# Block-sparse attention with a feed-forward layer: the preparation of the second sequence is issued in earlier steps

## The chip, the cores and the metric

One core of a Trainium2 chip runs the whole computation. Its engines work side by side and are told apart in the profile as PE (matmuls), PEld (the loading of weights into PE), DVE (VectorE), ACT (ScalarE), POOL (GpSimd) and SP (SyncE, which here issues nearly all transfers). The metric is the time of one execution on the device in microseconds (us). Lower is better. Every time below is of this kernel on one core, and "L723" is line 723 of the kernel.

## The reference

Four sequences of 768 positions, eight heads of 64 dimensions. Attention is block-sparse in blocks of 32: each block of queries sees its neighbours, the first and the last block, and three sampled blocks; the first and the last block of queries see everything. The heads are then joined to 512 features per position and go through two matrices with a leaky rectifier between them.

```python
def _attn_ref(q, k, v, sampled_blocks):
    ...
    scores = scale * np.matmul(q, k.transpose(0, 1, 3, 2))
    ...
    mask = np.abs(blk_i - blk_j) <= window
    mask = mask | (blk_i == 0) | (blk_j == 0) | (blk_i == n_blocks - 1) | (blk_j == n_blocks - 1)
    for qb in range(n_blocks):
        for kb in sampled_blocks[qb]:
            mask[qb * block:(qb + 1) * block, kb * block:(kb + 1) * block] = True
    ...
    attn = np.exp(scores)
    attn = attn / (np.sum(attn, axis=-1, keepdims=True) + 1e-09)
    return np.matmul(attn, v).astype(np.float32)

def _moe_ref(x, w_in, w_out):
    h = x @ w_in
    g = np.maximum(0.01 * h, h)
    return (g @ w_out).astype(np.float32)
```

The inputs and the result are float32. The kernel splits each operand into a high and a low float16 half and multiplies the halves, which is where most of its preparation comes from.

## The kernel before

**Steps.** The work is a list of 192 steps. A step is one unit: 64 queries of two heads (a head pair, `hp` 0 to 3) of one tile. Four head pairs make a tile (`T`), four tiles make an item, three items make a sequence, so a sequence is 48 steps: the first has steps 0 to 47, the second begins with step 48. For every unit PE forms scores (L714), DVE subtracts the mask and takes the maximum (L723), ACT takes the exponential (L735) and the high half of the normalised weights (L762), DVE the low half (L783), one transfer turns a pair of units around (L788), and PE multiplies by V (L815). Tile 0 of a sequence (steps 48 to 51 in the second) sees all 768 keys, so it needs no gathered keys but takes two parts per unit; each later tile works on 384 gathered keys.

**What a sequence needs beforehand.** Each of these is a Python generator that issues one piece and then yields a cost in "units" (about a microsecond of ACT or DVE each):

- queries, `prep_q`: half an item at a time, 128 positions, halves 0 to 23; halves 6 to 11 are the second sequence's. A square on ACT (L230), a sum across partitions on PE (L135), a scale on DVE (L149 to L158), the high half on ACT (L594), the low half on DVE (L596), a transposing transfer (L599) and two copies (L601, L602). The raw half is loaded by `load_q` into a single buffer.
- keys, `prep_k`: one head pair at a time, with the same pieces (L230, L135, L149 to L158, L564, L568, L570) and one transposing transfer into the tile `kt` (L574). The buffer of the split keys, `k16`, is single, so the next head pair's square waits for this one's transfer; the raw keys have two buffers. `kt` shares two buffers with `wbuf`, in which raw weights are decoded, so the second sequence's `kt` takes over the place of the first one's.
- values, `prep_v`: four squares, one sum, one scale, and then for each head pair the high half (L505), two low halves (L508) and a transfer to DRAM (L512), from which later tiles gather rows (L676, L683).
- weights, `prep_weights`: eight parts, decoded from raw words (L363 to L367) and split (L430, L435, L425 to L428). A credit of 1.8, 1.7 and from step 32 on 4.5 units a step sets how fast they are issued.

`gather_k` builds the keys of a tile: one DVE copy (L647) and six POOL copies (L656), issued from the step in which the tile before it begins. `start_gather` forces all four head pairs' keys to be complete first.

**The order.** A string of letters per step says in which order the pieces of a step are issued (`ord` up to step 47, `ord1` from step 48); "p" stands for `side_step`, "S" for the scores of the following units. `side_step` has a quota of 1.6 units in steps below 16 and of 1.2 units after that. It goes once through the list of open flows, queries first and the others in the order in which they were opened, and takes one piece from each as long as quota is left. A flow that is needed and not complete is forced through at that place (`until`). A scheduler then puts the instructions on the engines' queues by priority, 200 apart per step, as their inputs are ready in its own model of time; squares and sums of the weights have a priority 1500 higher. Each engine works through its queue in order, and so does SP's queue of transfers.

**The feed-forward part** comes in chunks (`ffn_h` L850, `ffn_o` L877), eight per item and 24 matmuls of L850 in each. The first two items go quarter by quarter as the weights' quarters are ready; from step 48 on one chunk is issued in every second step, by a table of due steps.

**The places that the change touches** are the driver loop (the calls of `start_q`, `get_k` and `start_k`), the line of "p" in it, and the sort in `side_step`. In the kernel before, the second sequence's keys are loaded in steps 26, 31, 36 and 41 and opened in 29, 34, 39 and 44; its first queries (half 6) are loaded in step 35 and opened in step 40; its values are loaded in 28 to 34 and opened in step 36.

Of the kernel before, what the change touches and what calls it, by code (L numbers as in the profile page):

```python
# [29 lines left out]
CFG = {  # L30
    "ahead": 3,
    "av_lag": 3,
    "bs": 1500,
    "early": 2,
    "even_at": 48,
    "even": 12,
    "flag": 1,
    "g": 2,
# [20 lines left out]
    "rmin": 0.0,  # L59
    "side": 1.2,  # L60
    "side0": 1.6,
    "spair": 1,
    "spread": 8,
    "v_at": 28,
# [8 lines left out]
def tile_block_sparse_attention_ffn(  # L73
# [508 lines left out]
    def prep_q(b, j, i, rq):  # L582

        nm = f"q{b}_{j}_{i}"
        ss = sm.tile([P, 1], F32, tag="ssq", name=f"ss_{nm}")
        qa = pa.tile([P, H, 2, D], F16, tag="qa", name=f"qa_{nm}", bufs=1)
        square(flat(qa)[:, :H * D], rq.rearrange("p h d -> p (h d)"), ss)
        yield 0.7
        yield 0.01
        pb = scale_sum(ss, 1, nm)  # L590
        yield 0.2
        inv, s = scale_of(pb, 1, nm)
        yield 0.4
        nc.scalar.activation(qa[:, :, 1, :], rq, AF.Copy, scale=s[:, :1])  # L594
        yield 0.7
        nc.vector.scalar_tensor_tensor(  # L596
            out=qa[:, :, 0, :], in0=rq, scalar=s[:, :1], in1=qa[:, :, 1, :], op0=ALU.mult, op1=ALU.subtract)
        qs = pa.tile([P, H, P], F16, tag="qs", name=f"qs_{nm}", bufs=2)
        nc.sync.dma_start_transpose(out=qs, in_=flat(qa))  # L599
        qxs = pa.tile([P, H, P], F16, tag="qxs", name=f"qxs_{nm}", bufs=2)  # L600
        nc.sync.dma_start(out=qxs[:D], in_=qs[D:])  # L601
        nc.sync.dma_start(out=qxs[D:], in_=qs[:D])  # L602
        last_sp["q"] = latest()
        qstack[b, j, i] = (qs, qxs, inv)
        yield 0.8
# [323 lines left out]
    flows = []  # L929

    def start(key, gen):
        gens[key] = gen
        flows.append(key)
# [21 lines left out]
    def side_step(amount):  # L955

        quota[0] = min(quota[0] + amount, 2 * amount)
        for key in sorted(flows, key=lambda a: a[0] != "q"):
            if quota[0] <= 0:
                break  # L960
            c = next(gens[key], "end")
            if c == "end":
                flows.remove(key)
            else:
                quota[0] -= c or 1.0
# [61 lines left out]
    def get_q(n):  # L1027
        if n < len(halves):
            if n >= CFG["rq"]:
                until(("q", *halves[n - CFG["rq"]]), lambda: halves[n - CFG["rq"]] in qstack)  # L1030
            rq[n] = load_q(*halves[n])

    def start_q(n):
        if n < len(halves):
            start(("q", *halves[n]), prep_q(*halves[n], rq[n]))
# [8 lines left out]
    def start_k(b, hp):  # L1044
        start(("k", b, hp), prep_k(b, hp, rk[b, hp]))
# [48 lines left out]
    step = 0  # L1094
# [44 lines left out]
    for u in units:  # L1139
        it, ui = u.item, u.k * NP + u.hp  # L1140
        b, nb = it.b, it.b + 1
# [2 lines left out]
            start_q(1)  # L1144
        if step == 6 or step % 8 == 3 and step > 8:
            get_q((step + 5) // 8 + 1)
        if step % 8 == CFG["q_at"] % 8:
            start_q(step // 8 + (2 if CFG["q_at"] < 8 else 1))
        if nb < B:
            g = it.j * 16 + ui  # L1150
            t = g - (CFG["k_at"] if b else CFG["k_at0"])
            every = CFG["k_every"] if b else 5
            if t % every == 0 and 0 <= t // every < NP:
                get_k(nb, t // every)
            if t % every == every - 2 and 0 <= t // every < NP:
                start_k(nb, t // every)
            t = g - CFG["v_at"]
            if t in (0, 2, 4, 6):
                load_v(nb, t // 2)
            if t == 8:  # L1160
                start(("v", nb), prep_v(nb))
# [18 lines left out]
        for w in CFG["ord1" if step >= CFG["ord1_at"] else "ord"]:  # L1180
            if w == "c" and c:
                ffn_act1(c)
            elif w == "m" and c:
                ffn_max(c)
            elif w == "g" and c:
                ffn_act2(c)
                oq.append(aq.popleft())
            elif w == "S" and step + 1 < len(units):
                ahead = units[step + 1:step + 3]
                if not CFG["spair"]:  # L1190
                    scores(ahead[:1])
                elif u.pi == 1:
                    if any(x.parts > 1 for x in ahead):
                        for x in ahead[:1]:
                            scores([x])
                    else:
                        scores(ahead)
                elif u.parts > 1:
                    scores(ahead[:1])
            elif w == "t":  # L1200
                while live[0] + u.parts > CFG["p"]:
                    if not pend_high and not pend_split:
                        norm_step()
                    high_step()
                    split_step()
                live[0] += u.parts
                unit_ttr(u)
            elif w == "x":
                unit_exp(u)
                if step >= CFG["even_at"]:  # L1210
                    last_exp[0] = latest()
                if u.pi == 1:
                    pend_norm.append(u.pair)
            elif w == "d":
                norm_step()
            elif w == "i":
                high_step()
            elif w == "s":
                split_step()
            elif w == "a":  # L1220
                av_step()
                if vq and vfree[0] and (vq[0][0], "ready") in scr:
                    start_gather_v()
            elif w == "v":
                ev_step()
            elif w == "b":
                do_out()
            elif w == "o":
                do_o(CFG["flag"] if hq or aq else 0)
            elif w == "p":  # L1230
                side_step(CFG["side0"] if step < 16 else CFG["side"])
                gather_step(2)
            elif w == "w":
                wcredit += [r for a, r in CFG["wr"] if step >= a][-1]
                now = tc.cur_priority
                if step < 16:
                    tc.cur_priority = now + CFG["wlate"]
                begin = len(nc.cur_bb.bb.instructions)
                while wcredit >= 1.0:
                    c = next(weights, "end")  # L1240
                    wcredit -= c if c != "end" else wcredit
                if 0 < step < 16:
                    behind(begin, last_ttr[0])
                tc.cur_priority = now
            elif w == "h":
                for i in range(n):
                    if i:
                        do_act()
                        do_o(CFG["flag"])
                    do_h()  # L1250
# [65 lines left out]
```

## Time and profile before

| | us |
|---|---|
| median of three runs | 850.7 |
| the three runs | 850.25 to 853.37 |
| the profiled execution, as timed | 851.52 |
| its span in the profile | 849.8 |

The profile belongs to the execution of 851.52 us: 849.8 us from the first to the last instruction, and 1.7 us around it. That execution is 0.8 us above the median of the three runs. The tables of windows in the prediction give, for each stretch of the span, how many of its microseconds an engine was busy, the number of instructions in brackets, the clock granted to TensorE as a share of full speed, and the mean busy share of the transfer engines (it can be over 1).

### The profile page before, as it was taken

How to read it: one execution, taken by the hardware profiler on the slowest of the kernel's cores; microseconds unless marked ns; L12 is line 12 of the kernel's file. 1: busy time of each engine (PE TensorE's matmuls, PEld its weight loads, DVE VectorE, ACT ScalarE, POOL GpSimd, SP SyncE). 2: the span in 40 equal slices, each digit the busy share in tenths (PEclk: the TensorE clock that was granted, in tenths of full speed). 3: DMA queues.
4: the chain of work that ended last, by engine and by line, in shares of the span. 5: the costliest groups of instructions: out<-in, count | busy, mean ns of one | idle time of the engine just before them, and what ended most of it. 6: DMA issues, size and time to landing. Idle time of an engine off the chain costs nothing.

```text
span 849.8 us, 20081 instructions
## 1 busy us (share of the span) xinstructions
PE 749.3 (88%) x7140; PEld 500.6 (59%) x7140; DVE 595.5 (70%) x1595; ACT 507.6 (60%) x1199; POOL 352.8 (42%) x472
## 2 busy tenths in 40 slices
PE   1666675857798999999999999998999999999997
PEld 1455543545465666666666666665666666667664
DVE  5768889898777976867777777678666776651221
ACT  5757678776445766767566667675657556551211
POOL 0218356433233464646343455454244545332221
PEclk9977778989799999999999999999999999999999
DMA  9979289998756999996969999969586766662000
GB/s 198 273 218 247 73 176 240 245 260 147 168 131 106 175 213 190 203 179 146 197 154 154 196 182 186 202 130 204 119 155 150 125 149 139 125 129 35 26 1 25
DMA packets 312004, 135.33 MB, mean 159 GB/s; under 512 B 279774, under 2 KB 292063, under 8 KB 311903
## 3 DMA queue, kind: packets, MB, share of 16 engines
q1 hardware_dynamic: 305262, 113.59, 67.2%
q0 software_dynamic: 6640, 20.45, 9.3%
q8 instruction: 56, 0.92, 0.5%
q14 instruction: 46, 0.37, 0.2%
HBM read 65.58 MB, written 12.58 MB: 92 GB/s over the span
## 4 chain that ended last, share of the span: by engine, by line
PE 70%; DMA 12%; DVE 10%; issue 3%; ACT 2%; SPq 2%; POOL 0%; POOLq 0%; ACTq 0%; DVEq 0%
PE h L850 27%; PE o L877 26%; PE s L714 8%; PE av L815 7%; DMA pt<-pp 3%; DMA wbuf<-in_moe_w_out_dram 2%; DMA qxs_q<-qs_q 2%; DMA qs_q<-qa_q 2%; DVE p L723 2%; DVE pp L783 2%; PE turn L773 2%; DVE W L365 1%; DVE W L435 1%; DVE W L367 1%; PE q_sum L135 1%
## 5 line engine op out<-in xcount | busy, mean ns | idle before, releaser
L877 PE MATMUL o<-W,g 128*128 128x512 f16 x1152 | 270.9, 381 | 6.4 <-DVE ob L898 4.2
L850 PE MATMUL h<-x,W 128*128 128x256 f16 x2304 | 274.2, 277 | 0.2 <-DVE x L833 0.2
L850 PEld LDWEIGHTS <-W 128*128 128x128 f16 x2304 | 225.0, 100 | 37.7 <-issue 3.9
L864 POOL TENSOR_TENSOR g<-ht,g 128x512 f16<-128x512 f32 x96 | 116.9, 1217 | 304.5 <-DVE g L863 254.6
L735 ACT ACTIVATE p<-p,mx 128x384 f32<-128x384 f32 x208 | 126.2, 607 | 158.7 <-DVE mx L723 123.0
L877 PEld LDWEIGHTS <-g 128*128 128x128 f16 x1152 | 108.7, 98 | 125.6 <-issue 10.8
L656 POOL COPY kg<-kt 128x256 f16 x264 | 135.0, 540 | 45.0 <-issue 15.4
L783 DVE SCALAR_TENSOR_TENSOR pp<-p,r,pp 128x384 f16<-128x384 f32 x188 | 120.4, 666 | 24.9 <-ACT pp L762 23.6
L762 ACT ACTIVATE pp<-p,r 128x384 f16<-128x384 f32 x188 | 104.2, 604 | 23.9 <-DVE r L747 10.2
L723 DVE CUSTOM_DVE_ANT_0 p<-s,em,nsc 128x384 f32<-128x384 f32 x176 | 102.0, 608 | 19.8 <-PE s L714 17.1
L683 POOL DMA_INDIRECT vg<-scr,rows x88 | 91.3, 1037 | 50.4 <-issue 20.3
L859 DVE SCALAR_TENSOR_TENSOR ht<-ht 128x512 f32<-128x512 f32 x96 | 67.8, 706 | 53.3 <-ACT ht L856 52.7
L815 PE MATMUL av<-pt,vg 128*64 128x128 f16 x2112 | 82.1, 226 | 10.1 <-DMA pt<-pp 9.6
L815 PEld LDWEIGHTS <-vg 128*64 128x64 f16 x2112 | 73.4, 114 | 27.4 <-issue 21.7
L714 PE MATMUL s<-kg,qs_q 128*64 128x384 f16 x352 | 66.2, 351 | 25.0 <-DVE mx L723 22.7
L856 ACT ACTIVATE ht<-h,gd 128x512 f32<-128x512 f32 x80 | 53.8, 672 | 57.3 <-PE h L850 54.7
L714 PEld LDWEIGHTS <-qs_q 128*64 128x64 f16 x416 | 27.0, 111 | 79.2 <-issue 53.7
L714 PE MATMUL s<-kg,qxs_q 128*64 128x384 f16 x352 | 64.0, 343 | 5.4 <-DMA qxs_q<-qs_q 5.4
L747 DVE RECIPROCAL r<-sum 128x2 f32<-128x2 f32 x96 | 15.4, 161 | 60.2 <-ACT sum L746 57.8
L863 DVE CAST g<-ht 128x512 f16<-128x512 f32 x96 | 41.8, 435 | 9.4 <-PE o L877 7.2
L735 ACT ACTIVATION_READ_ACCUMULATOR p<-p,mx 128x1 f32 x208 | 39.0, 187 | 0.0
L714 PEld LDWEIGHTS <-qxs_q 128*64 128x64 f16 x416 | 26.2, 114 | 20.8 <-DMA qxs_q<-qs_q 9.7
(138 smaller groups left out, 758.0 us busy)
## 6 DMA issues: line engine op xcount, KB each, us to landing
vg<-scr SPq DMA_DIRECT2D x33, 256.0 KB
qxs_q<-qs_q SPq DMA_DIRECT2D x48, 128.0 KB
v<-in_v_dram SPq DMA_DIRECT2D x32, 192.0 KB
scr<-v SPq DMA_DIRECT2D x16, 384.0 KB
W<-in_moe_w_in_dram SPq DMA_DIRECT2D x5, 1024.0 KB
rq<-in_q_dram SPq DMA_DIRECT2D x20, 256.0 KB
out_dram<-ob SPq DMA_DIRECT2D x20, 256.0 KB
rk<-in_k_dram SPq DMA_DIRECT2D x24, 192.0 KB
```

Source lines behind the costliest of these rows:

```text
L656: nc.gpsimd.tensor_copy(out=kg[:, :, slot * BLOCK:(slot + 1) * BLOCK], in_=kt[:, :, bass.ds(off, BLOCK)])
L683: nc.gpsimd.indirect_dma_start(out=vg[:n_, c, :], out_offset=None, in_=scr[b][:, :], in_offset=bass.IndirectOffsetOnAxis(ap=rows[:n_, c - ...
L714: nc.tensor.matmul(o, a, k, start=(n == 0), stop=(n == 1)))
L723: nc.vector.tensor_tensor_reduce(out=u.p[i], in0=u.sp[i], in1=kgs[u.b, u.T][1] if u.T else zero.to_broadcast([P, KEYS]), scale=u.nsc, scal ...
L735: nc.scalar.activation(u.p[i], u.p[i], AF.Exp, scale=-1.0, bias=u.mx[:, :1], accum_out=u.pair.sum[:, u.pi, i:i + 1])
L762: nc.scalar.activation(pp[:, 0, :], p, AF.Copy, scale=u.r)
L783: nc.vector.scalar_tensor_tensor(out=pp[:, 1, :], in0=p, scalar=u.r, in1=pp[:, 0, :], op0=ALU.mult, op1=ALU.subtract)
L815: nc.tensor.matmul(o, a, m, start=(c == 0 and l == 0), stop=(c == n - 1 and l == 1)))
L850: nc.tensor.matmul(c.ph[:, i], w, x, start=(d == 0 and m == 0), stop=(d == NP - 1 and m == 2)))
L859: nc.vector.scalar_tensor_tensor(out=c.t, in0=c.t, scalar=0.01, in1=c.t, op0=ALU.mult, op1=ALU.max)
L864: nc.gpsimd.tensor_tensor(out=c.g[:, 1], in0=c.t, in1=c.g[:, 0], op=ALU.subtract)
L877: nc.tensor.matmul(o, a, w, start=(c.first and i == 0 and m == 0), stop=(c.last and i == 1 and m == 2)))
```

## The change

- A setting `side1` of 2.0 is added: `side_step` gets a quota of 2.0 units in steps 28 to 47, where it had 1.2.
- The open flows are taken in the order queries, keys, values; before, queries came first and the others in the order in which they were opened.
- The second sequence's keys are loaded every four steps (26, 30, 34, 38) and opened in steps 28, 32, 36 and 40.
- Half 6 of the queries is opened in step 37 in place of 40. The other halves are opened in the steps that they had.

Nothing is added to or taken from what is computed; instructions are issued in another order.

```diff
+    "side1": 2.0,
...
     def side_step(amount):
 
         quota[0] = min(quota[0] + amount, 2 * amount)
-        for key in sorted(flows, key=lambda a: a[0] != "q"):
+        for key in sorted(flows, key=lambda a: "qkv".index(a[0])):
             if quota[0] <= 0:
                 break
             c = next(gens[key], "end")
...
-        if step % 8 == CFG["q_at"] % 8:
-            start_q(step // 8 + (2 if CFG["q_at"] < 8 else 1))
+
+        if step == 37:
+            start_q(6)
+        elif step % 8 == 0 and step != 40:
+            start_q(step // 8 + 1)
         if nb < B:
             g = it.j * 16 + ui
             t = g - (CFG["k_at"] if b else CFG["k_at0"])
-            every = CFG["k_every"] if b else 5
+            every = CFG["k_every"] if b else 4
...
             elif w == "p":
-                side_step(CFG["side0"] if step < 16 else CFG["side"])
+                side_step(CFG["side0"] if step < 16 else CFG["side1"] if 28 <= step < 48 else CFG["side"])
                 gather_step(2)
```

## The prediction

> **What bounds the kernel now.** First the page's busy shares, where PE is the busiest engine with 88%, then windows of the span, stage by stage. I cut them where the scores (next fence) show a border.
>
> ```profile
> span 849.8 us, 20081 instructions
> PE 749.3 (88%) x7140; PEld 500.6 (59%) x7140; DVE 595.5 (70%) x1595; ACT 507.6 (60%) x1199; POOL 352.8 (42%) x472
> ```
> ```profile
> core 0: us, PE busy (x) PEld busy (x) DVE busy (x) ACT busy (x) POOL busy (x), PEclk, DMA share, GB/s
> 137.00:196.00 59.00, 35.31 (x380) 24.06 (x380) 55.93 (x150) 46.92 (x109) 25.27 (x31) 0.86 1.14 239
> 196.00:246.00 50.00, 42.45 (x371) 29.13 (x370) 38.23 (x100) 23.78 (x44) 13.32 (x12) 0.90 0.77 150
> 246.00:284.00 38.00, 33.15 (x308) 19.30 (x308) 29.91 (x83) 22.73 (x59) 15.84 (x25) 0.96 0.59 115
> 284.00:300.00 16.00, 16.00 (x161) 11.06 (x161) 15.64 (x43) 10.78 (x26) 6.39 (x9) 1.00 0.99 183
> 300.00:850.00 550.00, 538.56 (x5166) 357.58 (x5163) 347.76 (x922) 314.07 (x762) 238.74 (x314) 1.00 0.72 142
> ...
> 370.00:458.00 88.00, 86.66 (x890) 57.14 (x888) 65.54 (x178) 59.50 (x147) 38.62 (x51) 1.00 0.84 170
> 565.00:653.00 88.00, 84.02 (x836) 54.79 (x834) 63.79 (x171) 56.13 (x136) 37.43 (x51) 0.98 0.74 158
> ...
> 196.00:284.00 88.00, 75.59 (x677) 48.43 (x674) 68.14 (x183) 46.52 (x102) 29.16 (x36) 0.92 0.69 135
> ```
>
> From 300 us on PE is busy for 538.56 of 550 us: whatever is won ahead of that comes out of the end nearly whole, since the same matmuls follow. In 137 to 196 (steps 28 to 47 by the order of L723) DVE is the bound: 55.93 of 59 us. Between them lies the change of sequences: in 196 to 284 PE idles 12.41 us (88 − 75.59) at a clock of 0.92. The two later changes of sequence, in windows as long, idle 1.34 and 3.98 us at 1.00 and 0.98. Those sequences are prepared well ahead; the second is not. Its scores show that:
>
> ```profile
> 192.86 0.33 PE L714 MATMUL s<-kg,qxs_q 128*64 128x384 f16 x2
> ```
> ```profile
> 227.19 0.58 PE L135 MATMUL wo_sum<-wo_ss,ones 128*128 128x1 f32 x2 [1.14 <-DVE wo_ss L204]
> 227.64 0.56 PE L135 MATMUL q_sum<-ss_q,ones 128*128 128x1 f32 x2
> ...
> 233.14 0.42 PE L135 MATMUL k_sum<-ss_k,ones 128*128 128x1 f32 x2
> 245.93 0.35 PE L714 MATMUL s<-kt,qs_q 128*64 128x384 f16 x2
> ```
> ```profile
> 173.41 0.62 ACT L230 ACTIVATE qa_q<-rq 128x512 f16<-128x512 f32 x1
> ...
> 195.74 0.83 ACT L230 ACTIVATE k_k<-rk 128x768 f16<-128x768 f32 x1
> ...
> 245.65 0.84 ACT L230 ACTIVATE k_k<-rk 128x768 f16<-128x768 f32 x1 [2.31 <-DMA kt<-k_k]
> ```
>
> For 53.1 us (192.86 to 245.93) no score is formed. Half 6 was squared at 173.41, but its sum runs at 227.64, in PE's queue right behind a weight sum which itself waited for DVE. The third head pair of keys was squared at 195.74 and summed only at 233.14; the fourth is squared at 245.65, behind the third's transfer. The transfers say what holds each:
>
> ```profile
> 169.00 5.41 POOL L656 COPY kg<-kt 128x256 f16 x6
> ```
> ```profile
> 175.53 2.12 SPq L574 DMA_TRANSPOSE kt<-k_k  x1
> ...
> 188.60 2.37 SPq L574 DMA_TRANSPOSE kt<-k_k  x1
> ...
> 224.72 5.23 SPq L512 DMA_DIRECT2D scr<-v  x3
> ...
> 235.37 1.23 SPq L599 DMA_TRANSPOSE qs_q<-qa_q  x1
> ...
> 240.19 1.51 SPq L602 DMA_DIRECT2D qxs_q<-qs_q  x1
> 241.75 1.56 SPq L574 DMA_TRANSPOSE kt<-k_k  x1
> ...
> 255.30 1.45 SPq L574 DMA_TRANSPOSE kt<-k_k  x1
> ```
>
> The first keys of the second sequence land right behind the first sequence's last gather (169.00 + 5.41 = 174.41, then 175.53): `kt` takes over that buffer. The four then follow each other through the single `k16`: 13.1 us from the first to the second, 53.2 to the third, 13.6 to the fourth.
>
> **The change part by part.** I counted by hand in which step each piece is issued; a flow gives one piece per pass at most.
>
> *Queries.* Half 6: square 40 → 37, sum 42 → 39, low half and transfers 43 → 42. On PE, sums and feed-forward chunks go in order of step as banks come free: the keys' sum of step 36 ran at 183.57, that of V (step 41) at 202.84, half 6's (step 42) at 227.64.
>
> ```profile
> 183.57 0.38 PE L135 MATMUL k_sum<-ss_k,ones 128*128 128x1 f32 x2 [0.85 <-ACT k_k L230]
> ...
> 202.84 0.28 PE L135 MATMUL v_sum<-ssv,ones 128*128 128x4 f32 x2
> ```
>
> Step 39 lies between the first two: some 195. From sum to first score the chain took 18.3 us (227.64 to 245.93), so the scores would begin near 213, 33 us sooner.
>
> *Keys.* Last pieces: 34, 39, 48, 48 → 33, 37, 41, 45; the forced run of seven pieces in step 48 goes. The first cannot land sooner than the last gather allows (175), the second follows at about 188 as now, and the third's square at 195.74 stays. Only its sum no longer waits 37 us; at 13.1 us a head pair (first to second) the third lands near 202 and the fourth near 215, where they took 241.75 and 255.30. Loading every four steps buys little: the raw keys have two buffers, and the fourth load waits for the second's low half anyway. Each load is 192 KB twice either way; it moves by 2 to 3 steps on a queue of transfers that is 1.14 busy in that window. I cost it at 0; bounds are −1 and +2.4 us (one transposing transfer of keys on SP, 2.37).
>
> *Values.* Last piece 51 → 49, and keys go first. The rate of 2.0 can't do more for them: one piece a pass from step 36 ends in step 49. V's last transfers were issued by 230 (224.72 + 5.23), and the first that needs V is this:
>
> ```profile
> 270.51 0.61 PE L815 MATMUL av<-pt,v 128*64 128x128 f16 x15 [0.65 <-DMA pt<-pp]
> ```
>
>  Thirty-three us sooner that would be 237, still behind V's 230. Cost 0, between −1 and +2 us by the same rows.
>
> *What is moved into the full stage.* What leaves 196 to 246 for steps up to 47 must find room on DVE. Prices:
>
> ```profile
> 185.31 0.16 DVE L158 RECIPROCAL k_s<-k_inv 128x1 f32<-128x1 f32 x1
> ...
> 187.56 1.01 DVE L570 SCALAR_TENSOR_TENSOR k_k<-rk,k_s,k_k 128x768 f16<-128x768 f32 x1
> ```
> ```profile
> 234.60 0.74 DVE L596 SCALAR_TENSOR_TENSOR qa_q<-rq,q_s,qa_q 128x512 f16<-128x512 f32 x1
> ```
> ```profile
> 225.72 1.15 DVE L508 SCALAR_TENSOR_TENSOR v<-v,v_s,v 128x384 f16<-128x384 f32 x2
> ```
>
> Half 6 is four small ones and L596: 4 × 0.16 + 0.74 = 1.4 us. Two head pairs of keys: 2 × (5 × 0.16 + 1.01) = 3.6. Three of V's low halves: 3.5. Together 8.5 us at most. But the keys can't be ready before 196 (`k16`, above), and V's scale runs behind its sum; so I take the queries' 1.4 us, rounded to 1.5, on the path. Range 0 to 8.5.
>
> *What comes back.* PE's 12.41 us of idle time fall to those of the worse of the later changes, 3.98: −8.4 us. DVE, too, has room: 88 − 68.14 = 19.9 us. The clock: 75.59 us busy at 0.92 are 69.5 at full speed. Halfway, at 0.96, they are 72.4: −3.2. Since the clock was below 1 in 565 to 653 too, with far fewer gaps, I take half of it, −1.6. Bounds: 0 and −6.1 (75.59 − 69.5).
>
> Sum: −8.4 − 1.6 + 1.5 = **−8.5 us**. The profiled execution goes from 851.5 (span 849.8 and 1.7 around) to 843.0; that execution stood 0.8 above the median of the runs, so the time I give is **842.2 us**.
>
> [...]
>
> **The rivals.**
>
> *Full.* The gap closes wholly: 12.41 of idle time and 6.1 of clock return, 18.5 us, less 1.5: 850.7 − 17 = 833.7. For it: 284 to 300 is already without idle time. Against: the weights' last split, which two quarters of the first items' last chunks need, ends at 239.4 by DVE's own queue.
>
> ```profile
> 239.14 0.28 DVE L428 COPY W<-wbuf 128x512 f16<-128x512 f16 x1
> ```
>
> *Same, by the weights.* Most of PE's idle time before 239 waits for the weights' DVE work and for output sums, not for scores:
>
> ```profile
> PE o L877 <- DVE ob L898: 4.2, 1, 4.2
> ...
> PE wi_sum L135 <- DVE wi_ss L204: 1.6, 1, 1.6
> ```
>
> An in-order queue holds early scores back there as well. Then only half of the 4.85 us of 246 to 284 (38 − 33.15) is won, less 1.5: −1, 849.7.
>
> *Same, by the sum.* The change doesn't do what it says: half 6 ends one step sooner only (42 for 43), and its sum again falls in behind the weights' squares, which have a priority of 7.5 steps more. Scores then begin near 246 as now: 850.7.
>
> *Slower.* One mechanism: DVE in 137 to 196. If all 8.5 us of moved work land there, the weights' decoding behind it in DVE's queue moves back by as much, and with it the last chunks that it gates, so the idle time of the seam stays and only the clock's 1.6 us returns: 850.7 + 8.5 − 1.6 = 857.6. It decides from the point at which L428 ends more than 8 us behind 239.4. For it: DVE at 95% in that stage. Against: `k16`.
>
> A row that bears on this rival:
>
> ```profile
> 195.99 1.27 DVE L435 SCALAR_TENSOR_TENSOR W<-W,wo_s 128x1024 f16<-128x1024 f32 x1
> 197.26 2.11 DVE L435 SCALAR_TENSOR_TENSOR W<-W,wo_s 128x1024 f16<-128x1024 f32 x1
> ```
> ```profile
> 196.22 2.06 POOL L864 TENSOR_TENSOR g<-ht,g 128x512 f16<-128x512 f32 x1 [1.13 <-DVE g L863]
> ```
>
> The same DVE instruction took 0.84 us more beside a POOL instruction. The second sequence's first gathers, six POOL copies a tile, would now meet the weights' splits (before 239) where they met none: six times 0.84 is 5.0 us at most on DVE, inside the range above. [...]
>
> **How the numbers follow.** A measurement of this kernel tells about 0.5% from no change, so faster means below 846.4 and slower above 855.0. Chances: the forecast 0.47 (836 to 846.4, from the clock's whole 6.1 and half of the rest of the idle time to half of the forecast); full 0.13; same by the weights 0.14 and by the sum 0.08; slower 0.18. So faster 0.60, same 0.22, slower 0.18. The range goes from 834 (full) to 856, which leaves out the upper half of slower and the lower edge of full.
>
> **What would show it.** Right: the gap without scores falls from 53.1 to some 20 us (10 to 30); q_sum near 195 and the fourth kt transfer near 215; in the 88 us behind the first sequence's last score PE idles about 4 us; L428 ends by about 241; PE stays over 97% busy behind it. Wrong: q_sum right behind wo_sum again (same by the sum); scores early but PE idle as long (same by the weights); steps 28 to 47 longer than 62 us and L428 beyond 247 (slower). What would make it wrong outside of these: the scheduler orders the later changes of sequence anew, where idle times of 1.34 and 3.98 us show what such an order is worth.

## The result and the profile after

| | before | after |
|---|---|---|
| median of 14 runs, us | 846.53 | 848.22 |
| lowest to highest, us | 842.10 to 853.37 | 843.02 to 854.96 |
| first profiled execution, as timed (span) | 851.52 (849.8) | 843.93 (842.2) |

After to before the ratio is 1.0069, 95% interval 1.0042 to 1.0096: by this ratio the change makes the kernel 0.7% slower, a small difference, but clear of no change. The ratio is formed from the fast executions alone, those less than 1.5% above the quickest of their kernel, and is not the ratio of the two medians, which is 1.0020. The forecast was 842.2 us and faster. The two first profiled executions lie 7.6 us apart in the direction opposite to the runs, so no stage may be read from this one pair alone; further down there are five profiles of each kernel.

The page of the changed kernel:

```profile
span 842.2 us, 20065 instructions
...
PE 748.3 (89%) x7140; PEld 502.7 (60%) x7140; DVE 593.4 (70%) x1595; ACT 508.3 (60%) x1199; POOL 353.9 (42%) x472
```

PE's work is the same (749.3 us before). The windows of the prediction, on the changed kernel:

```profile
137.00:196.00 59.00, 37.83 (x410) 27.45 (x410) 50.83 (x138) 43.78 (x102) 20.70 (x27) 0.69 1.14 249
196.00:246.00 50.00, 40.51 (x379) 27.80 (x380) 46.20 (x128) 31.09 (x62) 14.91 (x13) 0.99 0.73 160
246.00:284.00 38.00, 37.90 (x350) 24.08 (x349) 32.06 (x82) 22.14 (x57) 18.60 (x30) 0.97 0.60 106
...
196.00:284.00 88.00, 78.42 (x728) 51.88 (x729) 78.26 (x209) 53.23 (x119) 33.51 (x42) 0.98 0.67 136
...
300.00:842.20 542.20, 531.27 (x5092) 352.32 (x5089) 341.24 (x908) 308.88 (x750) 235.04 (x307) 0.99 0.71 141
```

In 196 to 284 PE idles 9.58 us (88 − 78.42), not the 4 of the forecast, and all but 0.1 of it now lies before 246. The longest wait there is this one, for a transfer of attention weights:

```profile
244.45 0.56 PE L816 MATMUL av<-pt,v 128*64 128x128 f16 x10 [3.67 <-DMA pt<-pp]
```

In 137 to 196 the granted clock fell from 0.86 to 0.69. So two things did not go as planned, one behind the seam's first score and one well ahead of the seam. First the seam, in PE's timeline:

```profile
194.63 0.33 PE L715 MATMUL s<-kg,qxs_q 128*64 128x384 f16 x2
...
196.27 0.36 PE L136 MATMUL q_sum<-ss_q,ones 128*128 128x1 f32 x2
...
213.94 0.52 PE L715 MATMUL s<-kt,qs_q 128*64 128x384 f16 x4
...
228.81 0.38 PE L136 MATMUL wo_sum<-wo_ss,ones 128*128 128x1 f32 x2 [0.92 <-DVE wo_ss L205]
229.05 0.36 PE L136 MATMUL k_sum<-ss_k,ones 128*128 128x1 f32 x2
...
250.47 0.35 PE L715 MATMUL s<-kt,qs_q 128*64 128x384 f16 x2
```

The gap without scores shrank from 53.1 to 19.3 us (194.63 to 213.94), and half 6's sum runs at 196.27. But the fourth head pair's sum now stands right behind a weight sum (229.05 behind 228.81), where half 6's sum stood before. Its key transfer follows at 239.68. DVE's copy of these keys waits for their landing until 245.51, and the scores of unit 51, the first that need them, run at 250.47. SP's queue of transfers shows both ends:

```profile
158.64 2.66 SPq L600 DMA_TRANSPOSE qs_q<-qa_q  x1
...
162.53 1.58 SPq L575 DMA_TRANSPOSE kt<-k_k  x1
164.21 0.93 SPq L602 DMA_DIRECT2D qxs_q<-qs_q  x1
165.19 0.59 SPq L603 DMA_DIRECT2D qxs_q<-qs_q  x1
...
202.06 1.56 SPq L575 DMA_TRANSPOSE kt<-k_k  x1
209.95 1.23 SPq L600 DMA_TRANSPOSE qs_q<-qa_q  x1
...
239.68 2.66 SPq L575 DMA_TRANSPOSE kt<-k_k  x1
```

The second thing is at the top of this fence. The first key transfer stands in SP's queue ahead of half 5's two copies, which units 40 and 41 of the first sequence need; the copies go out 5.6 us behind their transposition (164.21 − 158.64). In the kernel before, they went out 3.2 us behind it (168.25 − 165.03), and the key transfer came at 175.53:

```profile
165.03 1.25 SPq L599 DMA_TRANSPOSE qs_q<-qa_q  x1
...
168.25 0.58 SPq L601 DMA_DIRECT2D qxs_q<-qs_q  x1
168.87 0.59 SPq L602 DMA_DIRECT2D qxs_q<-qs_q  x1
```

PE's queue of the changed kernel at the same place:

```profile
163.72 0.90 PE L715 MATMUL s<-kg,qs_q 128*64 128x384 f16 x4
168.08 0.59 PE L136 MATMUL k_sum<-ss_k,ones 128*128 128x1 f32 x2 [3.46 <-ACT k_k L231]
168.53 4.96 PE L851 MATMUL h<-x,W 128*128 128x256 f16 x24
173.41 0.52 PE L715 MATMUL s<-kg,qxs_q 128*64 128x384 f16 x4
```

The scores of units 40 and 41 begin at 163.72 with the operand that is there (`qs`). The copies that make the second operand had left SP by 165.78 (165.19 + 0.59), but next in PE's queue is the second head pair's key sum, for which PE idles 3.46 us because the square has only just run (167.09 to 167.93), then 24 matmuls of feed-forward at a granted clock of 0.55 (4.96 us; 24 others take 2.78 us at 179.19, at 1.00), and only then the other half of the scores (173.41). PE takes them in this order in e4's profile too: 171.70, 172.14 and 177.35. From the mask step of unit 39 to that of unit 40 it took 18.6 us; before, 2.9. Some 10 us of the 18.6 are this passage of PE's queue (163.72 to 173.93); 5.5 lie ahead of it, where PE waits for a transfer of attention weights, and 2.9 behind it, where DVE has other work before the mask step. The 18.6 us are not all lost, for unit 39 itself comes 24.8 us behind unit 28, where it came 39.1 us behind it before.

### The profile page after: what moved, and what is told of

It reads as the page before. It is cut to its first block, busy times and chain, and to the rows that moved or that the text cites. A ratio compares the mean times of both kernels' runs of the same rounds, so it can differ in the third digit from the quotient of the medians.

```text
span 842.2 us, 20065 instructions
## 1 busy us (share of the span) xinstructions
PE 748.3 (89%) x7140; PEld 502.7 (60%) x7140; DVE 593.4 (70%) x1595; ACT 508.3 (60%) x1199; POOL 353.9 (42%) x472
## 4 chain that ended last, share of the span: by engine, by line
PE 61%; DMA 4%; DVE 4%; SPq 1%; issue 1%; ACT 1%; DVEq 0%; ACTq 0%
PE o L878 25%; PE h L851 23%; PE av L816 6%; PE s L715 6%; DMA pt<-pp 3%; DMA qxs_q<-qs_q 1%; DVE pp L784 1%; DMA qs_q<-qa_q 1%; DVE p L724 1%; DVE v L509 1%; PE q_sum L136 1%; DVE ht L860 0%; SPq L789 0%; SPq L602 0%; SPq L603 0%
## 5 line engine op out<-in xcount | busy, mean ns | idle before, releaser
L851 PE MATMUL h<-x,W 128*128 128x256 f16 x2304 | 273.6, 277 | 1.5 <-DVE x L834 1.2
L878 PE MATMUL o<-W,g 128*128 128x512 f16 x1152 | 271.3, 381 | 1.2 <-DVE ob L899 0.7
L851 PEld LDWEIGHTS <-W 128*128 128x128 f16 x2304 | 225.2, 100 | 38.8 <-issue 4.6
L878 PEld LDWEIGHTS <-g 128*128 128x128 f16 x1152 | 109.0, 98 | 120.3 <-issue 8.7
L724 DVE CUSTOM_DVE_ANT_0 p<-s,em,nsc 128x384 f32<-128x384 f32 x176 | 102.3, 610 | 21.4 <-PE s L715 17.8
L684 POOL DMA_INDIRECT vg<-scr,rows x88 | 94.2, 1070 | 44.6 <-issue 21.6
L816 PE MATMUL av<-pt,vg 128*64 128x128 f16 x2112 | 84.2, 228 | 13.5 <-DMA pt<-pp 11.0
L816 PEld LDWEIGHTS <-vg 128*64 128x64 f16 x2112 | 75.8, 116 | 30.3 <-issue 21.4
L715 PE MATMUL s<-kg,qs_q 128*64 128x384 f16 x352 | 66.7, 355 | 21.4 <-DVE mx L724 18.0
L736 ACT ACTIVATION_READ_ACCUMULATOR p<-p,mx 128x1 f32 x208 | 39.1, 188 | 0.0
```

The source lines that it names most:

```text
L684: nc.gpsimd.indirect_dma_start(out=vg[:n_, c, :], out_offset=None, in_=scr[b][:, :], in_offset=bass.IndirectOffsetOnAxis(ap=rows[:n_, c - ...
L715: nc.tensor.matmul(o, a, k, start=(n == 0), stop=(n == 1)))
L724: nc.vector.tensor_tensor_reduce(out=u.p[i], in0=u.sp[i], in1=kgs[u.b, u.T][1] if u.T else zero.to_broadcast([P, KEYS]), scale=u.nsc, scal ...
L736: nc.scalar.activation(u.p[i], u.p[i], AF.Exp, scale=-1.0, bias=u.mx[:, :1], accum_out=u.pair.sum[:, u.pi, i:i + 1])
L816: nc.tensor.matmul(o, a, m, start=(c == 0 and l == 0), stop=(c == n - 1 and l == 1)))
L851: nc.tensor.matmul(c.ph[:, i], w, x, start=(d == 0 and m == 0), stop=(d == NP - 1 and m == 2)))
```

## Where the lead went

The stages, cut at the mask steps (L723, L724) of units 28, 40, 48, 60 and 72. Kernel before:

```profile
137.29:179.28 41.99, 23.54 (x236) 14.94 (x236) 39.21 (x96) 32.60 (x76) 22.23 (x28) 0.84 1.16 226
179.28:246.49 67.21, 54.71 (x515) 38.43 (x514) 54.66 (x155) 38.30 (x76) 16.56 (x15) 0.90 0.84 180
246.49:295.05 48.56, 43.70 (x411) 27.15 (x411) 40.66 (x113) 30.03 (x76) 19.58 (x32) 0.96 0.68 129
295.05:335.06 40.01, 40.01 (x403) 26.63 (x402) 30.83 (x85) 26.25 (x65) 21.86 (x29) 1.00 1.08 201
```

Changed kernel:

```profile
133.47:176.86 43.39, 21.14 (x212) 15.02 (x212) 35.34 (x95) 33.51 (x79) 17.03 (x26) 0.57 1.11 250
176.86:218.79 41.93, 37.56 (x384) 25.98 (x383) 41.82 (x114) 29.41 (x60) 12.93 (x11) 1.00 0.94 193
218.79:281.09 62.30, 55.66 (x528) 36.14 (x525) 52.56 (x146) 35.97 (x84) 25.92 (x35) 0.97 0.63 129
281.09:327.25 46.16, 46.16 (x444) 30.58 (x440) 35.66 (x95) 28.21 (x68) 23.55 (x31) 1.00 0.96 192
```

Units 40 to 47 take 41.93 in place of 67.21 us: there is the gap that closed. Then units 48 to 59 take 62.30 in place of 48.56, and units 60 to 71, in which PE is never idle in either of these profiles, 46.16 in place of 40.01. A stage without idle time that grows at the same granted clock, 1.00 in both, has more work in it. These are the feed-forward matmuls, from the windows of L850 and then L877 in the kernel before (PE's busy time and the number of matmuls):

```profile
137.29:246.49 109.20, 31.45 (x240) 0.87 0.96 198
246.49:335.06 88.57, 29.46 (x254) 0.98 0.86 161
...
137.29:246.49 109.20, 22.11 (x88) 0.87 0.96 198
246.49:335.06 88.57, 33.43 (x140) 0.98 0.86 161
```

and of L851 and L878 in the changed one:

```profile
133.47:218.79 85.32, 18.70 (x144) 0.78 1.03 222
218.79:327.25 108.46, 39.65 (x347) 0.98 0.77 156
...
133.47:218.79 85.32, 14.26 (x60) 0.78 1.03 222
218.79:327.25 108.46, 41.65 (x168) 0.98 0.77 156
```

From unit 28 to unit 48 the changed kernel needs 85.32 in place of 109.20 us, a lead of 23.9. But 96 matmuls of the first kind and 28 of the second are not done by then: 32.96 us of feed-forward work (18.70 + 14.26) against 53.56 (31.45 + 22.11). Of the 23.9 us, 20.6 are work put off. It is done behind unit 48, where there is 81.30 us of it against 62.89, and the lead goes. On this queue, which is the bound here, scores that came sooner were no gain in themselves: of the 23.9 us, 4.0 are left at unit 72 in this pair (197.77 − 193.78). A gain is only what takes away idle time or makes the same matmuls shorter, as with the 24 above (4.96 us at a granted clock of 0.55, 2.78 at 1.00).

Five profiles of each kernel (those of the table on top, e1 and e4, and e13 to e18, all below) give the means; "lead" is how much earlier than before the changed kernel reaches a unit, counted from the mask step of unit 28:

| | before: mean (the five) | after: mean (the five) |
|---|---|---|
| timed, us | 845.97 (851.5, 842.1, 845.5, 848.1, 842.6) | 845.41 (843.9, 849.0, 846.5, 844.2, 843.4) |
| start to unit 28, us | 135.1 (132.8 to 138.2) | 133.4 (131.7 to 135.1) |
| units 28 to 40, us | 42.7 (41.1 to 44.4) | 46.1 (43.4 to 50.3) |
| of it PE idle | 15.9 (14.4 to 18.5) | 24.6 (22.2 to 27.5) |
| units 40 to 72, us | 152.3 (149.8 to 155.8) | 149.5 (148.2 to 150.8) |
| of it PE idle | 16.1 (13.6 to 17.4) | 9.5 (8.2 to 11.0) |
| unit 72 to the end, us | 514.2 (512.9 to 515.3) | 514.7 (512.9 to 517.8) |
| granted clock | 0.954 (0.949 to 0.960) | 0.946 (0.943 to 0.951) |
| lead at unit 39, 40, 48, us | | 13.3, −3.4, 17.8 |
| lead at unit 51, 60, 72, us | | 8.2, 5.1, −0.6 |

The idle times do not overlap between the kernels in either stage. PE won 6.6 us of idle time in units 40 to 72 and lost 8.7 in units 28 to 40. In the profiled executions that is why the forecast gain is not there. In units 28 to 40 PE waits 3.3 to 5.1 us for the second head pair's key sum in each of the five profiles after, 4.0 us in the mean, and in none of the five before. The waits ahead of the multiplications by V are 5.5 us longer in the mean; what causes that is not traced.

## The experiments

All ratios are to the kernel before, run beside it on the same chip. Each diff is against the kernel before unless it says otherwise; the line numbers of these kernels are then those of the kernel before. The quoted expectations call theories by words in capitals and give each its numbers.

| run | what | median us | ratio (95%) |
|---|---|---|---|
| e1 | before, again | 846.85 | 1.002 (0.9983 to 1.0057) |
| e4 | after, again | 850.15 | 1.0075 (1.0035 to 1.0114) |
| e2 | keys | 860.13 | 1.0196 (1.0139 to 1.0253) |
| e5 | queries | 863.6 | 1.0205 (1.0153 to 1.0258) |
| e7 | queries and keys | 859.25 | 1.0178 (1.0118 to 1.0237) |
| e6 | rate | 853.8 | 1.0076 (1.0035 to 1.0118) |
| e3 | queries and rate | 851.55 | 1.0071 (1.0029 to 1.0113) |
| e8 | queries and rate, again | 850.34 | 1.006 (1.0022 to 1.0099) |
| e9 | whole, first two keys opened late | 850.35 | 1.0107 (1.0066 to 1.0148) |
| e10 | whole, other key steps | 846.17 | 1.0037 (1.0004 to 1.0069) |
| e11 | before, with repeated matmuls | 849.03 | 1.0034 (0.9996 to 1.0072) |
| e12 | after, with repeated matmuls | 851.84 | 1.0053 (1.0013 to 1.0093) |

**The two kernels again (e1, e4), unchanged.**

> The kernel before, unchanged, against itself: what the comparison says of no change. Every theory expects a ratio of 1.000 with an interval of some 0.3% to either side. Its profile is a second execution of the same instructions as in the profile of before: if stages of steps 0 to 27 differ by 4 us or so between the two profiles, then 4 us of the 7.6 us between the profiles of before and after are such spread and not the change.

> The whole change once more on the same chip as the three others. All theories but SPREAD expect 0.4 to 1% slower than before; SPREAD expects within 0.3%. Its second profile shows whether the stall of 18.6 us between units 39 and 40 comes with every execution (KEYS expects over 10 us again) and how far PE's idle time of 9.6 us in the 88 us behind the first sequence's last score is its own.

e1 bounds what this measurement tells: 1.002, an interval of 0.4% to each side. e4 repeats the result, 1.0075; the medians are 850.15 and 844.73 us there.

**One part at a time.** e2 takes only the keys' steps, e5 only half 6's, e6 only the rate:

```diff
-            every = CFG["k_every"] if b else 5
+            every = CFG["k_every"] if b else 4
```
```diff
-        if step % 8 == CFG["q_at"] % 8:
-            start_q(step // 8 + (2 if CFG["q_at"] < 8 else 1))
+        if step == 37 or step % 8 == 0 and step != 40:
+            start_q(6 if step == 37 else step // 8 + 1)
```
```diff
-                side_step(CFG["side0"] if step < 16 else CFG["side"])
+                side_step(CFG["side0"] if step < 16 else 2.0 if 28 <= step < 48 else CFG["side"])
```

The change's other line, which sorts the flows, is in none of e2 to e10. In the whole change and in e9 it moves nothing: the kernel with it and the one without it build into the same instructions in the same order. At the quota of 1.2 (e2, e7) and in e10 it would have moved some.

> The key loads every four steps alone (queries, order and rate as before). Theory KEYS (the earlier keys put the second sequence's first key transfer in front of the copies of half 5 of the queries on SP, and the second key sum in front of the scores of units 40 and 41 on PE, so that the first sequence's last units wait): slower than before by 0.7% or more, with a stall of over 10 us between units 39 and 40. Theory FULL STAGE (what the queries and the rate of 2.0 move into steps 28 to 47 costs): within 0.3% of before. Theory SPREAD (no part has an effect, executions differ): within 0.3%.

> Half 6 of the queries from step 37 alone; keys every five steps, quota 1.2. It takes none of the keys into steps 28 to 47. Theory GIVE-BACK (advancing the second sequence's scores does shorten PE's idle time in the seam by 3 to 8 us, but work of PE is put off and more of the execution goes at half clock, which costs about as much or more): within 0.5% of before, PE's idle time over the whole span lower by 2 to 5 us than the 95 to 100 us of the two profiles of before, its busy time higher by 3 us or more. Theory RATE (the quota of 2.0 is what costs): faster by 0.3 to 1%. Theory QUERIES (half 6 ahead is what costs): slower by 0.7%, as with the rate.

> The quota of 2.0 in steps 28 to 47 alone. GIVE-BACK: within 0.5%. RATE: slower by 0.7%, as with the queries. QUERIES: within 0.3%.

All three parts cost time alone: 2.0, 2.1 and 0.8%. Queries alone show why the rate had to go up with them. PE's timeline of e5:

```profile
246.68 0.28 PE L135 MATMUL k_sum<-ss_k,ones 128*128 128x1 f32 x2
...
262.51 0.53 PE L714 MATMUL s<-kt,qs_q 128*64 128x384 f16 x2 [7.73 <-DMA kt<-k_k]
```

and its queue of transfers:

```profile
241.95 7.90 SPq L512 DMA_DIRECT2D scr<-v  x4
...
254.98 2.38 SPq L574 DMA_TRANSPOSE kt<-k_k  x1
...
268.45 1.41 SPq L574 DMA_TRANSPOSE kt<-k_k  x1
```

At a quota of 1.2, half 6's pieces take the place of keys and values: the third and fourth key transfers come at 254.98 and 268.45, where they took 241.75 and 255.30 before, and V's last transfers end at 249.85 in place of 229.95. PE then stands idle for 7.73 us before the third head pair's scores. Units 40 to 72 took 167.9 us (mean of the five before: 152.3). With the keys alone (e2), the stall ahead of unit 40 is there by itself: 15.6 us from unit 39 to 40, and 51.6 us for units 28 to 40. So it comes from the keys' steps, not from the queries or the rate. It is not all of e2's 2%: in its trace V's last transfers end at 258.70, some 29 us later than before. The rate alone (e6) costs as much as the whole change, 1.0076; in its profile there is no stall, but PE idles 21.4 us in units 40 to 72 (16.1 before). KEYS foresaw e2, and e6 fits RATE; e5's 2.1% lies outside all that the theories gave.

**Two parts (e7, e3, e8).** e7 has the first two diffs, at the old quota. e3 has the second and the third, with the keys at every five steps; e8 is e3 again.

> Half 6 from step 37 and keys every four steps, at the quota of 1.2 (values end three steps later than in before: step 54 for 51). Keys alone were 2% slower and the whole change 0.75%. If the stall between units 39 and 40 (18.6, 19.4 and 15.6 us in the three profiles with earlier keys, 2.9 in those without) comes from the keys, it stands here again with over 12 us. If what makes keys alone so slow is that half 6 then comes last (step 43, behind the keys on SP and PE), this kernel is about as the whole change, 0.4 to 1.2% slower; if it is the lower quota (values late), it is 2% slower.

> Half 6 of the queries from step 37 and the rate of 2.0, with the keys every five steps as before. Theory KEYS: the early scores of the second sequence come without the stall, so faster than before by 0.3 to 1%; the scores' gap between units 47 and 48 is about 20 us and that between units 39 and 40 under 6 us. Theory FULL STAGE: slower by 0.7%, as the whole change. Theory SPREAD: within 0.3%.

> The kernel of queries and rate once more, on the chip of this call. It was 0.71% slower, though its profile was one of its quickest executions (844.8 against a median of 851.6). All theories but SPREAD expect 0.3 to 1.1% slower again; SPREAD within 0.3%. Its second profile is to show in which stage a common execution of it loses what the first profile does not: GIVE-BACK expects PE's busy time over 752 us and its idle time under 95.

e7 costs 1.8%. Its stall between units 39 and 40 is 11.0 us, where over 12 were expected, and V's last transfers end at 263.66, so without the rate the values are late here too. e3 and e8 keep half 5's copies ahead of the first key transfer, and their units 28 to 40 took 39.8 and 39.4 us with 14.4 and 13.7 us of idle time, where the kernel before took 41.1 us or more with 14.4 or more. All the same they are slower, by 0.7 and 0.6%, where KEYS expected e3 to be 0.3 to 1% faster. Their seam wins no idle time: in units 40 to 72 PE idles 14.7 and 18.0 us (16.1 before). The parts do not add: 2.1% for the queries and 0.8% for the rate are 0.65% together, and the keys (2.0% alone) add nothing to that.

**Undo the stall alone (e9).** The whole change without its sort, and the first two head pairs are opened in steps 29 and 34 as before:

```diff
+            if g in (26, 30, 34, 38) if not b else t % every == 0 and 0 <= t // every < NP:
...
+            if g in (29, 34, 36, 40) if not b else t % every == every - 2 and 0 <= t // every < NP:
```

> The whole change, but the first two head pairs of the second sequence's keys are opened in steps 29 and 34 as in before (loads in 26, 30, 34, 38; the other two opened in 36 and 40). Only the early opening of those two is undone, and with it the first key transfer stands behind the copies of half 5 on SP again. Theory WATERBED (the change does take 6 to 8 us of PE's idle time out of units 40 to 72, but the early first keys put 7 to 8 us into units 28 to 40, with a clock of 0.57 and 0.61 there against 0.84 and 0.75): units 28 to 40 take 39 to 43 us with 14 to 18 us of PE idle, the mean clock is 0.948 or more, units 40 to 72 take 146 to 151 us, and the time is 0.993 to 1.001 of before, so below the 1.007 of the whole change. Theory RATE (all kernels with the quota of 2.0 were 0.6 to 0.8% slower, whatever else they had): 1.006 to 1.008 again, with whatever times by stage.

Its windows of units 28 to 40 and 40 to 48:

```profile
131.88:175.14 43.26, 27.61 (x260) 17.41 (x255) 39.86 (x96) 32.37 (x76) 20.65 (x29) 0.78 1.06 222
175.14:219.38 44.24, 35.51 (x358) 25.70 (x359) 40.46 (x113) 30.13 (x63) 11.62 (x9) 0.84 0.95 231
```

The stall is gone: 3.1 us from unit 39 to 40, and idle time of 15.65 us (43.26 − 27.61) as before the change. The gap without scores stayed closed: 44.24 us for units 40 to 47. But units 40 to 72 idle 13.6 us, where the changed kernel idles 9.5 in the mean: with the stall undone, most of what the seam had won is gone too. Over units 28 to 72 PE idles 29.2 us, 2.8 less than the mean before. The time did not come back, 1.0107: WATERBED, which expected these stages and 0.993 to 1.001, has the stages right and the time wrong, while RATE's 1.006 to 1.008 reaches into the interval. The profiled execution (842.26 us) is the quickest of the twelve; the others took 846.0 to 857.4. So the stall explains a part of where the idle time of the profiles went, but it alone does not explain the 0.7% of the runs.

**Other key steps (e10).** As e9, but loaded in 26, 31, 36, 39 and opened in 29, 34, 38, 41.

> As the kernel of queries and rate (keys loaded in 26, 31, 36 and opened in 29 and 34 as in before), but the third and the fourth head pair are opened in steps 38 and 41 in place of 39 and 44, the fourth loaded in 39. It moves only the late keys, on which units 50 and 51 waited (unit 51 at 254 us in both profiles of queries and rate). WATERBED: units 28 to 40 as in queries and rate (39 to 41 us, 14 us of PE idle), unit 51 some 5 to 15 us sooner, time 0.993 to 1.003 of before. RATE: 1.006 to 1.008.

1.0037, the best of the changed ones, and still not faster than before. Its profiled execution was the longest of its twelve (853.2 us; the others 840.1 to 850.4), so no stage is read from it.

**Is it the clock (e11, e12)?** The executions of the changed kernel had a lower mean granted clock than those of the kernel before. To raise it without moving any other instruction, the finished program gets four repeats of the first score matmul of each unit from 28 to 47. They write the same values to the same place. e11 does this to the kernel before, e12 to the changed one:

```diff
     with _tile.TileContext(nc, schedule_with_timeline_sim=True) as tc:
         tile_block_sparse_attention_ffn(tc, *args)
+    repeat(nc, 28, 48, 4)
```

> The kernel before, with its instructions in their own order on every engine; only in units 28 to 47 the first score matmul of a unit (64 queries, 384 keys) is done four times more with the same operands, before the others add to it. That is 80 more matmuls of some 0.17 us at full clock, 13 us of PE work in a stretch in which PE idles some 24 us. They hold no other engine's work but PE's. Theory CLOCK (what is lost is PE's time at half clock: the executions of the changed kernel had a mean granted clock of 0.945 against 0.953): the clock here rises above 0.955, and the time stays within 0.5% of the kernel before or falls a little, 0.995 to 1.003. Theory ORDER (the loss comes from which engine waits for which, and the clock only follows it): the 13 us delay the scores where PE's queue is late, the ratio is 1.003 to 1.015, with whatever clock.

> The changed kernel with the same four repeats of the first score matmul in units 28 to 47, its instructions otherwise in its own order. It is to be compared with e11 on the same chip. CLOCK: with repeats its mean clock comes within 0.003 of e11's, and its time within 0.3% of e11's, so the 0.7% are gone. ORDER: the time stays 0.5 to 1.0% above e11's even at an equal clock. If the clock stays 0.007 under e11's, the repeats do not reach the place where the clock is lost, and nothing is told.

Units 28 to 40 of e11, then of e12:

```profile
134.73:178.06 43.33, 31.00 (x290) 20.41 (x287) 37.79 (x95) 32.63 (x76) 22.86 (x29) 0.89 1.16 236
```
```profile
133.06:182.12 49.06, 28.54 (x286) 19.19 (x286) 35.53 (x94) 33.45 (x79) 17.17 (x27) 0.79 1.15 243
```

The clock in this stage rose from 0.57 to 0.79 in the changed kernel, and over all executions the two are equal: a mean of 0.9586 and 0.9583. So are the times: means of the runs that the ratios use of 850.04 and 850.03 us, a ratio of 1.0000 with an interval of 0.4% to each side (from the spread of the 12 and 11 executions). ORDER, 0.5 to 1.0% at an equal clock, is not borne out by that, though units 28 to 40 still take 5.7 us more (49.06 and 43.33); by the table's two ratios e12 lies 0.2% above e11, so ORDER's lower edge is not firmly excluded. CLOCK is not shown by it either: the repeats raised the changed kernel's clock by 0.012 to 0.015 (from the 0.946 and 0.944 of its two sets of executions) and made it no faster that these intervals could tell (1.0053, with 1.0069 and 1.0075 without them), and with them the kernel before is at 1.0034, which its interval does not tell from 1 (CLOCK expected at most 1.003, ORDER at least that). What can be said is that with equal clocks no difference between the two kernels could be told.

**Where the 5 us lie (e13 to e18).** Three more profiles of each kernel, unchanged.

> The kernel before, unchanged, for a third profile. LOCAL: over the profiles of each kernel the stretch from the mask step of unit 28 to that of unit 72 is 3 to 6 us shorter here than in the changed kernel, with the rest equal within 2 us. ELSEWHERE: that stretch is equal within 2 us, and the loss stands ahead of it or behind it. REPEATED: the whole spans are equal within 2 us in the mean.

> The changed kernel, unchanged, for a third profile. LOCAL: units 28 to 72 take 196 to 200 us in the mean against some 193 to 195 of the kernel before. ELSEWHERE: units 28 to 72 are equal within 2 us, the stretch ahead of unit 28 or behind unit 72 is 3 to 6 us longer. REPEATED: all three stretches are equal within 2 us in the mean.

> The kernel before, for a fourth profile: as for the third. The stall between units 39 and 40 stays at some 3 us, and the granted clock lies between 0.945 and 0.965.

> The changed kernel, for a fourth profile: as for the third. The stall between units 39 and 40 is 18 to 20 us again under each theory, as it comes from the order of the queues, and the granted clock is 0.940 to 0.950.

> The kernel before, for a fifth profile. LOCAL: units 28 to 72 in the mean of the five 3 to 6 us shorter than in the changed kernel. ELSEWHERE: equal there within 2 us, with the loss ahead of unit 28 or behind unit 72. REPEATED: the five spans equal within 2 us in the mean.

> The changed kernel, for a fifth profile: LOCAL, units 28 to 72 3 to 6 us longer in the mean of the five; ELSEWHERE, equal there within 2 us and longer ahead of it or behind it; REPEATED, equal spans within 2 us.

The table of the section before has the result. Units 28 to 72 differ by 0.6 us (194.95 and 195.55), unit 72 to the end by 0.5, and the whole time by −0.6 us. That is what REPEATED expected. With spreads of 3.9 and 2.3 us among five, the interval of that difference is about 5 us to each side, so these profiles do not exclude the 3.6 to 8.1 us of the runs firmly. The stall between units 39 and 40 was 19 to 21 us in each of the three of the changed kernel and 2.9 in each of the others: it belongs to the order of the queues.

**What stays open.** For the profiled executions the traces show where the gain went. Why the timed executions are 0.7% slower, while the five profiled ones are not, they do not show. No trace of the other executions exists, and the stall alone does not carry it (e9). The rate is a suspect that was not followed up: it alone costs as much as the whole change (e6), and of the kernels with it only e10 (1.0037) and e12 (1.0053) came out below 1.0060; how it would cost this is not shown. The clock goes with the time. Among the executions that the ratios use, a clock lower by 0.01 goes with 4.1 us more in the kernel before (94 executions) and 5.8 us more in the changed one (25), and the two mean clocks lie 0.007 apart. That it is the cause is not shown: e11's repeats raised the clock by 0.008 over the executions beside it, and its time did not fall.

## Why the prediction was wrong, point by point

- **The gap of the scores: right.** 53.1 to 19.3 us, with half 6's sum at 196.27 (some 195 foreseen) and the first scores at 213.94 (near 213). What falls on this path by the prediction's own steps came out.
- **The third key transfer: right by luck, the fourth: wrong.** 202.06 (near 202) and 239.68 (near 215). The four transfers do not follow each other at 13.1 us: they begin at 162.53, 171.77, 202.06 and 239.68. The third head pair's square ran at 178.13, not at 195.74 as foreseen, and its transfer took 23.9 us from there; an earlier start and a longer chain cancelled out. The step "at 13.1 us a head pair" took the chain through `k16` as the only thing that holds it. The fourth's square ran at 207.12, but its sum stood in PE's queue behind wo_sum until 229.05: the hold that the prediction had named for half 6, and left out for this one. At unit 51, the first to need it, the lead has shrunk from 17.8 to 8.2 us.
- **"Loading every four steps buys little … I cost it at 0": the step that failed.** It priced the loads on a queue of transfers, between −1 and +2.4 us. What moved with them was not priced: the opening of the first two head pairs, one and two steps sooner. That puts the first key transfer ahead of half 5's copies on SP and the second key sum into PE's queue between two halves of the scores of units 40 and 41. Measured: 8.7 us more idle time and 3.4 us more time in units 28 to 40, in the mean of five profiles; 4.0 us of that idle time are the wait for the second key sum. This step is not the whole miss: e3 and e8 leave the keys' steps as they were and are no faster either, because without them the seam wins no idle time. "The first cannot land sooner than the last gather allows (175)" held as a rule and failed as a time: the first sequence's last copies of keys ended at 161.75, before 174.41, and the transfer followed at 162.53.
- **Idle time −8.4 us: near in size over units 40 to 72, too large in its own window, and wrong as a gain.** In units 40 to 72 it fell by 6.6 us in the mean. In the prediction's own window, 196 to 284, it fell only from 12.41 to 9.58: the 4.2 us for output sums are down to 0.7, but 3.67 us for a transfer of attention weights and 1.68 us for half 6's copies have come in. And taken over units 28 to 72 it rose, from 32.0 to 34.1 us (15.9 + 16.1 and 24.6 + 9.5).
- **The clock −1.6 us: right in its place, wrong in the sum.** In 196 to 284 the granted clock rose from 0.92 to 0.98. In 137 to 196 it fell from 0.86 to 0.69, and over the whole execution from 0.954 to 0.946. In the stage with 22.25 of 43.39 us idle it was 0.57, and 0.50 from 137 to 170; before, with 18.45 of 41.99 us idle, it was 0.84. The prediction counted the clock only where idle time went, not where it was put. What share of the clock comes back with the gaps, 1.6 us or the 6.1 of "full", was the author's estimate, and how the clock follows idle time is not shown: in e9's stage it was 0.78 with 15.65 us idle.
- **DVE, +1.5 us and the rival "slower": the right stage with the wrong engine.** From unit 28 to unit 47 it took 64.5 us, as that rival had said (over 62), but DVE was busy for 50.83 us in 137 to 196 against 55.93: it was not full, and its longest waits there were for ACT (3.5 us in three waits for the weights that ACT decodes). The last split of the weights ended at 241.5, not beyond 247, so the mechanism of that rival, weights that come late, did not set in. Of the two rows behind that rival's price of 0.84 us, the shorter DVE instruction (195.99, 1.27 us) ran beside the POOL instruction too, for 1.04 us, and the longer one for 1.02: that the meeting costs the 0.84 us is not shown. The row of the last split:

```profile
241.01 0.48 DVE L429 COPY W<-wbuf 128x512 f16<-128x512 f16 x2
```

- **"Whatever is won ahead of that comes out of the end": right, but the lead of the scores was not won.** From 300 us on PE is busy for 531.27 of 542.2 us, 98%, as foreseen. What is won on such a queue is idle time, and there was none left over.
- **Values at 0: right with the rate, and only with it.** Without it they end 20 us later (e5). "The rate of 2.0 can't do more for them" left out that it keeps the moved queries from pushing keys and values back.

## What to carry to other kernels

When one engine's queue is the bound, as PE's is here with 98% busy from 300 us on, count the gain of a change as its idle time over the whole stretch that the change touches, from the first instruction that moves to the point where the engine is full in both versions (here 32.0 us before and 34.1 after, units 28 to 72); an earlier first result with the work around it put off looks like a lead and is none (here 20.6 of 23.9 us). A piece of preparation that is opened one step sooner takes along its sum and its transfer, and each must be placed by hand into the queue that it enters, with the name of what stands behind it. Take several profiles of each version before reading a stage, since two of the same program can differ by more than the change (here 842.1 and 851.5 us).

## What was not expected of the hardware

- Executions of one program differ by more than the effect here: on one chip the kernel before took 836.7 to 855.2 us in 29 executions, and the change is 0.7%. Part of it lies in the first stretch, in which both kernels have the same instructions in the same order: it took 131.7 to 138.2 us over the ten profiles.
- Eighty more matmuls in a stretch with idle time raised the mean granted clock of the changed kernel from 0.944 to 0.958 (e4 and e12) and won no time that the intervals could tell (1.0075 and 1.0053).
